# Another issue table and other prices in the planner's account, in a fused attention and gated feed-forward kernel

## The chip, the cores and the metric

The kernel runs on one core of a Trainium2 chip. The metric is the device time of one execution in microseconds (us). Engines are named as the profile names them: PE is TensorE's matmul, PEld its weight load, DVE is VectorE, ACT is ScalarE, POOL is GpSimd, SP is SyncE, which issues most of the DMAs.

## The reference

The input x is 2048 tokens of 512 features, and all is float32. It is normalized over the features, and the normalized rows go through softmax attention with 32 heads of 16 and through a gated feed-forward network with 1792 hidden features. The two results are multiplied and added to the input:

```python
def _A_ref(x, wqkv, wo):                       # H = 32 heads, Dh = 16
    qkv = (x @ wqkv).reshape(B, S, 3, H, Dh) ...
    scores = einsum("bhqd,bhkd->bhqk", q, k) * Dh ** -0.5
    p = softmax(scores, axis=-1)
    return einsum("bhqk,bhkd->bhqd", p, v) ... @ wo

def _B_ref(x, w1, w3, w2):                     # F = 1792
    h = silu(x @ w1) * (x @ w3)
    return h @ w2

xn = layernorm(x)
return x + _A_ref(xn, wqkv, wo) * silu(_B_ref(xn, w1, w3, w2))
```

## The kernel before

**Precision.** A float32 number is split into a rounded part and a remainder ("hi" and "lo", both of the fp32r type), and a product is made of three matmuls: lo x hi, hi x lo, hi x hi. Queries and keys hold the parts of their 16 features stacked on 64 rows, so that one matmul of 64 rows does all three.

**Prologue** (the first 160 us). The input is normalized, transposed and split; queries, keys and values are made from it and written to DRAM; weights stream in.

**Main stage.** Two pieces of work that don't need each other share PE. The first is attention. It goes in 32 phases, two (halves of the queries) for each pair of heads. A phase has 64 units of kind m (lines 388 and 390: a block of scores of 128 queries by 512 keys is made, and VectorE reduces it to row maxima), 64 units of kind s (lines 624 and 627: scores the other way round, with the maximum folded in as two more rows, and ScalarE's exponential), and 16 value blocks v (line 637: four matmuls of 17 columns, one in each quarter of the array's columns, that add the exponentials times the values into one bank called pv). The maxima of a phase come before its exponentials; between them lie a small chain (max_rows: VectorE, ScalarE, VectorE, then a DMA). After a phase, take_out copies pv, and a generator of six steps divides by the sums: DMAs, a reciprocal on VectorE, DMAs again, one multiplication and two splitting instructions on POOL (lines 658 to 662), and the store.

The second is the feed-forward network, in units of kind f (line 855). A product takes 12 (gate, up) or 21 (down) pairs of matmuls, each with half of the 128 rows of the contraction. After a gate product ScalarE takes a tanh and a copy out of the bank, and POOL multiplies; after an up product ScalarE copies, and POOL multiplies and splits into hs. Down products read hs. POOL also splits all weights (lines 320 and 321).

**Lanes.** A matmul of kind f, s or m uses 64 of the array's 128 rows, so two run side by side: a lane for the upper rows and one for the lower. A value block uses all rows.

**The order.** PE's order is written out: ORDER_OF_ISSUE, a string of 8598 letters. A small letter is a half in lane 0, a capital one in lane 1, v a value block, o a piece of the output projection (at the end). The loop at the end of the kernel function reads a letter, first lets side work out (settle, small, tend), and then emits the letter's matmul; a letter that isn't possible yet goes on a list and is tried again at each letter.

**The account.** Whether a letter is possible, which of the seven PSUM banks it takes, and when side work is written into the engines' queues is decided while the program is built, by a class Model that keeps a clock per lane and a "free at" time per engine. SLOT is the time of a half, TURN the time lost between halves and a value block, VALUES the time of a value block, COST the time of a standard piece of work on an engine and DONE what is added until it is known to be done. `mod.work(engine, start, cost)` books work and returns its end. On the chip, every engine runs its own queue in the order written, and semaphores enforce the dependences; a wrong account makes no wrong result, only waits.

Of the kernel before, what the change touches and what calls it, by code (L numbers as in the profile page):

```python
# [62 lines left out]
    "fFMvMsfSMfFsfFmSfFfMFsMffSffMFfFMfsFsFfmFfFFfFMSffMfFsfSmfFFsFmsFfFMsFFfmSfmFFfmFfMMmvvMsMffSFfSfFms"
    "FfFMffSmFFsmFFfSfmFfSFfSfFsFmSsvvSsmMsSvvMsFmSfFfFsFmFsFfSmfFFsmFFsFfMfSffMfFfMSfmMvvvmSMmSsvSFffMSf"
    "fMfSffFMfSfmSFfFsmfSfFMFsfFmsFFfFsmFfFFMsfFmSfFmFFsfMFfsFFmsFFfFmmMfFmSvvsMSmSmvsMMsfMfSvMssMMsvfMfM"
    "sMmMvvMsSffFMffSfMFsfFMfFsmFfSFfmFFsfSfMsFfFmFFffMSfFffMSfsFmFsFFfmSfFmfSFfmFSffFFFmmmFmMvvvvMsmFfSF"
    "sFfFmSFfSfmfFfSMFsFfmsFFMfsFFfMffMfMsMvvvMsMfSffSfFMfSfFmsFfFsFMsFfFmSFffSmfFFsfFmFSSmvvSmFmsFFfSfFm"
    "FsFmsFFffSfMSffFMsfFFmFfSfSfSffMmMvvmMsMmMvvvMfSfMffSSfMfSffMffSfMSffMfsFFMfsFFsfMFfFsfMFsfmFsFFMfsf"
    "FSfmFFsfFMsfFMfFFsmfFSfFmfMFmFfMmvvvMsMmSsvmSSfmFFsfFFmSfFFmMfsFfSffFMsFFfsFmfSFfMfSffMSFfsFfMSffFmF"
    "sFfMsfFFMfFmsFSmvvSmSsmMvSmSfmFFMvvvmSSfmfFfSmfSFmsFfFMfFsSffMfFSfMfFfsFfMsFsFMfFfFsfMFsfFMsfFmFsFfM"  # L70
    "fFfFMsSmvvmSsFmSFmvmSmSmSvmSfSFmFffSFmFsfFSmFfFsmFfSfFMfFsFmsFmFfFsFFmSffFFmfSsFmFMvvSsmFsSmvvMmsSmS"
    "vsMmFsFsFfFFmsFfFfMSfMfFsMffFSfFfMfMfMfmMvvsMfSfMSfFffMfFmSfFSfmFFsfFmFsFmFsFfMfFsFfMMmvvSmsSMmvvmSS"
    "fMffFSffMfSfFmFfSFmFsfFFmsFmFsFfFSfsFMfMsvvsSSmmSvvsMFmsFFfFfSfMfsFsFMfFfFsfMfSfFmSfFSffMfFfFMFFfSff"
    "MfSsmFfFsFmFsFfMsfFFmSffFmFMfmFmMvvvMfSsMfFsFffFFmsFMfsFfFfSmFSfMffFsFMfFfffFMfSfMFfSFfSfmsFsMfFFfmS"
    "FfmFsFFfmFFmmFsMFvvSsMmmMvvfMfSfMMffSFfsfSFmfFsFmsFfFMsfFFsMfFFfFmSmfSmvvvsMsSmMvSmFsmFsFmFFfFsFffSM"
    "fSfsFMfFfmFSfFfSfmMfFsSvvSmSsMsvvSsmMsMvSfMfSffMfFSfSfMfsfFMfSFfmSFfsFmFsfFFmFsFfmFFfMfSFffMsfFsFMfF"
    "sFmFsFfmFSFfmSfFFfmfMFmmMvvvmFSfmFSsfFFfFmFsMfSfFfFmsFFmSfSfFfMffSfFsSvvvFsMSfFmsFfFmsFFfFsmFfSFmFsF"
    "ffMSfFffMFfMfMMsvvSfMfSfMfSfffSfMSffMFsFfmsFfFsFMfFsfFMFsfsMFfFffMMsFfMmvvsMFsMmMvvvsMMffSfSffMfSfMf"
    "SfMfsFfFsMFfsFmfSFfMfSfFmSfFSfmfFSfFmSFfsMFfsFfMFsfFmFsFmFFsFmFmFsSvmmSmMvvMmMmsSvvSmMsSmvmFFsFsmFFs"
    "FmfSfFfMFfsFmFsFmFFsFfmSFfSfmFsfFmSFfMffSfFMfFffMfMfMMfmMvvvmSMsMsFvMsfSfMffSfMfSfMffSfMsfFFsMfFFsmF"  # L80
    "SffMFsfFmFsFFmfSfSFfmfSFfMSffFmFsfFMsFfFFmFmmFmSvvvSssSSsvvvvMsFfFsSmFfFmSFfFsfSmfFfFmSFfmFSfFFsfMFf"
    "sFmfFSmfFfsFFFmsFFfFMsFfmFfFmSfFfSmFSfFfmFsFmFsFfFMfSfSfMsvvvvsMMmsSvmSFsmFSmvsMFffSfMSFffMsfFSmfFSf"
    "FsMfFffMSFffFsmFFfMSFfffMsFmFsFsfFfMFsfFSmFfMfFsfFMfFFmsMsmvvMmmSMvvvmSSmfSFffFFmSFfmfFSfMfSFfmFsfFf"
    "SMFsfFmfFfFFMSfffMSfSffMfsFFmFssFmFFfMfsFFsfFFmmFmMFvvvsMmSsMvSmfMmMvvMssSmfFfFFmsFFfSmFffSfMfSfFmSF"
    "fFfmSFffFFMfSffMSffSfMfFsFmFsFfmFsFmFsFFfmFSmfFMmvvsMsMmMvvMfsMSfmSvSmMssMvSmFmsFFfsFFmSFfFmsFSffMff"
    "SfFMSfFfsMffSFfMffFMffSfSFfMfFsFmsFFfmSfFmFsFFfFmFmmFmSvvSmsMSmvMsfMSfSmvMmSssMvMssFmFmFsFFfFsfFMfsF"
# [58 lines left out]
def kernel(ctx: ExitStack, tc: tile.TileContext, x, wqkv, wo, w1, w3, w2, out):  # L145
    nc = tc.nc
# [148 lines left out]
    mod = Model()  # L295
# [1042 lines left out]
```

## Time and profile before

| | |
|---|---|
| median of 3 runs | 1714.51 us (1714.36 to 1714.62) |
| the profiled execution | 1715.0 us |
| its span, first to last instruction | 1713.2 us |
| granted PE clock | 1.000 |
| busy share: PE, DVE, ACT, POOL | 100%, 84%, 72%, 45% |
| HBM traffic | 89 GB/s over the span |

In the profile, a group or piece of the timeline names its line, the engine, the operation and the tile written and read (`mp<-m` is the reduction of a bank m into mp). A matmul's length in the timeline is its latency; matmuls overlap, so what they cost is read from the distances of their starts. A value block appears as 8 matmul records.

### The profile page before, as it was taken

Reading aid. Unit: us, or ns where it says so; the run is one execution under the profiler, and the core shown is the slowest. Engines: PE = TensorE matmul, PEld = TensorE weight load, DVE = VectorE, ACT = ScalarE, POOL = GpSimd, SP = SyncE. Lnnn points to the kernel's source line nnn. Section 1 sums busy time; section 2 is a strip of 40 time slices with the busy share of each in tenths; the row PEclk is TensorE's granted clock in tenths of the full one; section 3 lists DMA queues with packets and bytes.
Section 4 is the critical chain, followed back from the end, with each engine's and each line's share of the span. In section 5 each row is a group of like instructions: output and inputs, shape, how many; then the busy total and the mean of one; then the engine's idle time right before and its main releaser. Section 6 shows DMA issues by size and latency. Waiting matters only on the chain.

```text
span 1713.2 us, 35632 instructions
## 1 busy us (share of the span) xinstructions
PE 1706.2 (100%) x13204; PEld 1093.8 (64%) x13204; DVE 1447.2 (84%) x2477; ACT 1233.2 (72%) x2408; POOL 764.2 (45%) x793
## 2 busy tenths in 40 slices
PE   9999999999999999999999999999999999999999
PEld 7877666666666666665656666666666656665466
DVE  7567998989898888899979898978999899779835
ACT  4223787787787877787787877887887777778962
POOL 4102754355545560656266525562556336642201
PEclk9999999999999999999999999999999999999999
DMA  8757213132333221232323213233422223131712
GB/s 284 249 205 206 66 40 71 45 76 64 71 105 72 79 55 37 68 69 73 99 80 69 73 30 73 56 70 109 81 59 67 58 55 100 45 106 55 244 61 99
DMA packets 146478, 155.37 MB, mean 91 GB/s; under 512 B 41472, under 2 KB 100864, under 8 KB 143328
## 3 DMA queue, kind: packets, MB, share of 16 engines
q1 hardware_dynamic: 145440, 152.04, 32.1%
q8 instruction: 104, 1.70, 0.4%
q10 hardware_dynamic: 864, 1.05, 0.2%
q14 instruction: 70, 0.57, 0.1%
HBM read 107.97 MB, written 44.02 MB: 89 GB/s over the span
## 4 chain that ended last, share of the span: by engine, by line
PE 97%; DVE 1%; POOL 1%; DMA 1%; issue 0%; SPq 0%; ACT 0%; POOLq 0%; DVEq 0%
PE f L855 27%; PE pv L637 27%; PE m L388 16%; PE e L624 15%; PE m L504 2%; PE e L194 2%; PE e L198 2%; PE e L196 2%; PE o L194 1%; PE o L198 1%; PE o L196 1%; DVE mp L390 1%; PE m L477 0%; DMA ks<-qk 0%; PE o L1086 0%
## 5 line engine op out<-in xcount | busy, mean ns | idle before, releaser
L390 DVE TENSOR_REDUCE mp<-m 128x1 f32<-128x512 f32 x2048 | 1286.4, 683 | 171.7 <-PE m L388 110.9
L627 ACT ACTIVATE pt<-e 128x512 f32<-128x512 f32 x2048 | 1071.5, 605 | 276.6 <-PE e L624 157.0
L624 PE MATMUL e<-qs,ks 64*128 64x512 f32 x2048 | 713.0, 410 | 0.1
L388 PE MATMUL m<-ks,qs 62*128 62x512 f32 x2048 | 710.9, 415 | 0.0
L637 PE MATMUL pv<-pt,vt 128*17 128x512 f32 x4096 | 491.0, 595 | 0.0
L388 PEld LDWEIGHTS m<-ks,qs 62*128 62x128 f32 x2048 | 338.4, 184 | 148.4 <-DVE mp L390 48.6
L624 PEld LDWEIGHTS e<-qs,ks 64*128 64x128 f32 x2048 | 341.5, 184 | 142.9 <-ACT pt L627 48.4
L637 PEld LDWEIGHTS pv<-pt,vt 128*17 128x17 f32 x4096 | 93.7, 96 | 237.0 <-issue 229.8
L855 PE MATMUL f<-xtl,wh 64*128 64x512 f32 x488 | 174.2, 393 | 0.0
L855 PE MATMUL f<-xth,wh 64*128 64x512 f32 x488 | 172.9, 393 | 0.0
L855 PE MATMUL f<-xth,wl 64*128 64x512 f32 x488 | 172.2, 394 | 0.0
L740 POOL TENSOR_TENSOR h<-g,h 128x512 f32<-128x512 f32 x56 | 72.1, 1288 | 213.7 <-ACT h L736 213.5
L855 PE MATMUL f<-wh,hs 64*128 64x512 f32 x496 | 158.1, 393 | 0.0
L855 PE MATMUL f<-xth,xel 64*128 64x512 f32 x408 | 148.9, 394 | 0.0
L855 PE MATMUL f<-xtl,xeh 64*128 64x512 f32 x408 | 148.8, 392 | 0.0
L855 PE MATMUL f<-xth,xeh 64*128 64x512 f32 x408 | 146.1, 392 | 0.0
L855 PE MATMUL f<-xeh,hs 64*128 64x512 f32 x400 | 127.1, 394 | 1.0 <-POOL hs L742 1.0
L321 POOL TENSOR_TENSOR wl<-wr,wh 128x512 fp32r<-128x512 f32 x92 | 118.4, 1287 | 7.7
L320 POOL TENSOR_SCALAR wh<-wr 128x512 fp32r<-128x512 f32 x92 | 56.9, 619 | 109.9 <-PE e L624 59.0
L321 POOL TENSOR_TENSOR xel<-wr,xeh 128x512 fp32r<-128x512 f32 x76 | 97.8, 1287 | 6.3
L855 PE MATMUL f<-wl,hs 64*128 64x512 f32 x248 | 91.1, 391 | 0.0
L855 PEld LDWEIGHTS f<-wh,hs 64*128 64x128 f32 x496 | 85.9, 185 | 6.5 <-issue 2.5
(175 smaller groups left out, 2016.6 us busy)
## 6 DMA issues: line engine op xcount, KB each, us to landing
wr<-in_B_w_dram SPq DMA_DIRECT2D x168, 256.0 KB
qs<-qk SPq DMA_DIRECT2D x186, 64.0 KB
ks<-qk SPq DMA_DIRECT2D x90, 128.0 KB
qk<-sh SPq DMA_DIRECT2D x32, 256.0 KB
qk<-sl SPq DMA_DIRECT2D x32, 256.0 KB
v<-vrow SPq DMA_DIRECT2D x16, 272.0 KB
xin<-in_A_x_dram SPq DMA_DIRECT2D x16, 256.0 KB
g<-part SPq DMA_DIRECT2D x16, 256.0 KB
```

The costliest lines, as they stand in the source:

```text
L194: nc.tensor.matmul(ps, lhs[1], rhs[0], start=first, stop=False)
L196: nc.tensor.matmul(ps, lhs[0], rhs[1], start=False, stop=False)
L198: nc.tensor.matmul(ps, lhs[0], rhs[0], start=False, stop=last)
L320: nc.gpsimd.tensor_scalar(hi, t, 1.0, 1.0, op0=ALU.mult, op1=ALU.mult)
L321: nc.gpsimd.tensor_sub(lo, t, raw(hi))
L388: nc.tensor.matmul(ps, qs[p % 2][64 * h:64 * h + KM, q0:q0 + P], ks[p % 2][64 * h:64 * h + KM, c * 512:(c + 1) * 512], start=True, stop=True)
L390: nc.vector.reduce_max(mp[p, half][:, h, qt, c:c + 1], ps, axis=AX.X)
L624: nc.tensor.matmul(ps, ks[p % 2][64 * h:64 * h + KR, k * P:(k + 1) * P], qs[p % 2][64 * h:64 * h + KR, q0:q0 + 512], start=True, stop=True)
L627: nc.scalar.activation(pt, ps, AF.Exp, scale=DH ** -0.5)
L637: nc.tensor.matmul(pv[32 * j:32 * j + VW, :], vt[2 * p // GH][:, key, 2 * p % GH + j % 2, :], pt, start=key < 2 if last else k == 0, stop= ...
L740: nc.gpsimd.tensor_mul(h2, g, h2)
L855: nc.tensor.matmul(ps, left[r], right[r], start=starts and lane == 0, stop=ends and lane == 1)
```

## The change

Two things change in the text.

1. The table ORDER_OF_ISSUE is replaced as a whole. Both tables have 8598 letters, with the same count of each kind. Counted in the texts:

| in the table | before | after |
|---|---|---|
| f and F, s and S, m and M | 4032, 2048, 1984 | 4032, 2048, 1984 |
| v, o | 512, 22 | 512, 22 |
| runs of neighbouring v | 268 | 253 |
| of these with 1, 2, 3, 4, 5, 6 blocks | 103, 107, 42, 12, 3, 1 | 83, 107, 45, 11, 6, 1 |
| stretches of halves between v or o | 278 | 265 |
| surplus of one lane over the other, added over the stretches | 144 | 150 |
| letters after the last m | 106 | 119 |

2. The account's numbers change, and it gets two bookings that it didn't have: for a phase's outputs, 0.18 on VectorE at the reciprocal and 3.3 on POOL at the multiplication and split. The instructions of these steps are the same.

```diff
 ORDER_OF_ISSUE = (
-    "fMSffMMsSfFfMfSfFsSffMffMfSffSfMSffMsfsFfMsfFMfsFfFMsFfFmSfFFmsFFmmMvMmmFMmvvvSmsMFfSfFffMSffMfSfsFF"
...
-    "sSsoovvosSsSSsovvSsSsSsoosSsSSsvvvsSSssSoSssSSsosSsSSsvvvsSsSsSooSsosSoSsvvSsSsoooSsSssSoooovvvvvv"
+    "FSMfsfMfMSffSMfffSfMSfMfffSfMSfsffMfsMFsFfmFsfFMsfFmFsFFFmsFfMfmMfFsMvvvMsMfSfSfFffMsFFfmFsMfFSffFfM"
...
+    "SvvvSsSsSsoSsSsSsoosSsSsSvvvvvsSsSsSsoooSssSSsvvvSsSssSosSSsSsvvSssSSsooSoossSosoooSvvooosSssSvvvv"
 )

     class Model:
-        SLOT, LOAD, TURN, VALUES, CLEAR, LATENCY, NOTICE = 0.232, 0.1, 0.097, 0.858, 0.983, 0.44, 0.054
-        COST = {"act": 0.495, "dve": 0.605}
-        DONE = {"act": 0.107, "dve": 0.078}
+        SLOT, LOAD, TURN, VALUES, CLEAR, LATENCY, NOTICE = 0.2335, 0.1, 0.097, 0.866, 0.983, 0.44, 0.054
+        COST = {"act": 0.495, "dve": 0.6}
+        DONE = {"act": 0.107, "dve": 0.083}
...
-                self.there[i] = mod.work("pool", mod.now, 1.9) - 0.1
+                self.there[i] = mod.work("pool", mod.now, 1.96) - 0.1
...
                     nc.scalar.activation(th, ps, AF.Tanh, scale=0.5)
-                    mod.work("act", lanes.begins + mod.LATENCY, 0.6)
+                    mod.work("act", lanes.begins + mod.LATENCY)
...
-                        mod.work("pool", ready, 1.9)
+                        mod.work("pool", ready, 1.96)
...
-                        made[i] = mod.work("pool", ready, 3.2)
+                        made[i] = mod.work("pool", ready, 3.3)
...
                         nc.vector.tensor_add(y, y, ps)
-                        free_at[lanes.at_bank[i]] = released[i] = mod.work("dve", ready, 0.7)
+                        free_at[lanes.at_bank[i]] = released[i] = mod.work("dve", ready)
...
-                        soon("pool", mod.work("act", ready, 0.6), i, lambda ready: times(ready, th))
+                        soon("pool", mod.work("act", ready, 0.5), i, lambda ready: times(ready, th))
...
-                        soon("sync", mod.work("pool", ready, 1.9) + 0.3, i, lambda ready: nc.sync.dma_start(
+                        soon("sync", mod.work("pool", ready, 1.96) + 0.3, i, lambda ready: nc.sync.dma_start(
...
             if c[2] == 0:
-                c[0] = mod.work("dve", mod.now, 0.25)
+                c[0] = mod.work("dve", mod.now, 0.15)
             elif c[2] == 1:
                 c[0] = mod.work("act", c[0], 0.2)
             elif c[2] == 2:
-                c[0] = mod.work("dve", mod.now, 1.15)
+                c[0] = mod.work("dve", mod.now, 0.95)
...
                 c[0] = mod.now + (LATER if c[2] < PHASES - 4 else SOON)[c[3]]
+                if c[3] == 1:
+                    mod.work("dve", mod.now, 0.18)
+                elif c[3] == 4:
+                    mod.work("pool", mod.now, 3.3)
...
             nc.scalar.copy(sums[j][0], pv)
-        pv_free = mod.work("act", begins + mod.VALUES + 0.3, 0.6) + mod.NOTICE
+        pv_free = mod.work("act", begins + mod.VALUES + 0.3) + mod.NOTICE
```

More of the change, by code (lines that the diff above doesn't have):

```diff
@@ new lines @@
+    "MfSfmFSfFFsfMSffFmfFSmFsfFFmSFffFmFsFmmSvvsMmMSsvvMsmSsFmFvMmsSsMvvmSsSmMvmSsMFfFffSfMsFffMSfSfFFmFs"
+    "FfmSfFMfsFfFfMfFSfMfSFffMsfmFsFfMFsmFFfsFfMFsFmFfMmfFMFmvvvvmSSFFsmffFmSfFfSmFfSfMsFfFfsMfFFsMffFFfM"
+    "fSfMFfSfSFfmsfFFmfSfMfSFffMsFmFsFFfFmFmFmmMvvvMsmSsMvSmfFsMFfSfFmFsFfSmfFFsMfsFfFMsFfmFFffMfMfSMfSmv"
+    "vmMsMsMvvfMSfMfSfSffMSFffMfSffMfSfMfSfmFsFfsFmFFsfFmSfFMfSfFsfFFmSfFsFmFsfFMSfffFMsfFSmFFfmFFfmMMsvv"
+    "mSmSmSvFmFsSsMmvmMMssMvvvmSFmsFsFFsFmFFfmFFsmfFSfSFfmfFFsmFSffFMsfFfSMfFfSmFFFffMfSSfFMfffMfMMfMfmMv"
@@ new lines @@
+    "vvsMSmsfFfFmsFFmfFSffMSSfMfFsfFffMsFFmFsFfmFSfFmFsFffSMsfFFfMsfFMfFfSffMMsvMmmSSmvvFmmSFsSmvMmsSmSvs"
+    "MFsmFsFmFFsFfFfSmFfFsFmFsfFMffSmFsFFfMfSfmFSffMFfsFFmMsvmMMsMsvvvmSsMmMvvSmmSFfFsFffMFsFfmSfFmFfSfMf"
+    "FsFfMfSFfmFmMFFfmMFvvmSmSfsfFFmsFfFSmfFfSfMsFfFMfSfMffSfSfFfmFFMfFfSmsFfFsMfFFsfMsFFfMsfFfMsFFfFsfFm"
+    "MmMvvvsMMsMsvmSmFSsFmvSmmSMmvvmSfSMfffSfFMSffmFFsFfMsFFsfMffFSmFsfffFMFSfMffFMsfFfSmFFsFmFsFmfFSfmFS"
+    "fFfFsFmSfsMvvMsSsmSvvvvsMFFsmFFsFmFsfFfSmFfSfMffSfFMSffMSffsFFfMFfffMSFFffMsfFsmFSffMFsFfmFsFfMsFFfF"
@@ new lines @@
+    "mFsfSSsvvvmMmMSsvvSmsSmFfFfFFmSffFSfMfsFFmsFfFMfSfSfFmFffFMfSffMfSfMfFSffSmfFSfMsFfFmsFFmFsFfsFFmFsF"
+    "mMvvsMMmmSvvsMFfmSsFFffMSffMfFSfFmSffmFfSfSFFmFfsmFfFFfMfSfSfMfFsFmfFFsFmFsFsMFffMFsFfFmMmFfMmvvvmSs"
+    "MSmFvvMssMMsvvfSMffSfMfSfSfmFsFFmFfFsfMFsSfFmFffFMfFssFmMvmSsMmMvvsMfSfSMffFFmFsFfSmfFsFMsfFFsMfFfSm"
+    "FFfMfMfmFMFsvvMssMffSfFfMSffFsMFfsFFmSffFmSfFmFsFFmfFFfSSfMmvSmSmSmvmSFMsfMMfvvvMffSfMSfSffMfSffMfSf"
+    "MsfmFsFmFfFsFmfFSmfFSfFMfsFffSMsFfFmFsFfMsFfFmFsFMfsFFfMffSMfsSvvvvvSmFsFmFmFsFsFffFSmFfsFfMfFSfMfFs"
@@ new lines @@
+    "MfsFFffMsFFmfSFfFsfMsFFfmSfFfMSffFMfSffMSmvvmMSsSmvvMsMffSSfFffMsFFfmSfFSfmFfFfSmFFsfMfSSFffmFsFmFSf"
+    "FfmFSffSSMfFmfFsFfFmFFmFssvvvsMsMmSvmFFsmFFsFmsFFmsFFFsmFFsFfmfFfSMfFsmFfFsFMSfMfFfsFfMSffMfFsSvMsMs"
+    "MmvvSmmSMmvvmSmFsFFsFfFmSffFMfSfMfFsFffMSfMfsFmFFfFFsfMsMvFvmSmsfFSffmSFFfSmffFSfMFsfMfSfFmSfmFFfFmF"
+    "mMsvvSmMmmMvvvmSfSfMFfSfFmfSFmfFSfmFsFmFFsmFFfSfFfmFfSMfFMsvsMfMsFffSfMfFmSFfFsFmsFfFmFsfFSMffSffMFf"
+    "FfFMSfffSmFsfFMfFFsmFFsfFmSfFmFsfFfMFfmMmMvvvmMsMsMvvMsMsSmvSmFfmSsfFfFSmFFfmSffSfFMSffFmfSFFmsFffMf"
@@ new lines @@
+    "FfFMSfSffFfMFsFmFsFfmFsFFmsFfFmSffFFMffmSmSvsMMssMvvsMMsMsvvMsMssMvSmfMsFfFfSFmsFFSfmFfSfmFfSfFMsFfs"
+    "FfMfSFfMfFfFSfMffSmfSfFMsfFFmsFfFmFSfFmFsfFMfmFmFmMvvvSmSmMmvvmSSmsMvMsFsfMfSFffMSffFsMfFsFFmFfsFfMs"
+    "FmFfSfFfFMFfFSffMfSffFSmsMfsfFFmFsFfMsFsFFfFmsFmMvSmfSfMsMvvvFsMmfSFfSFfSmFfSfmFsfFFmFsFmFsFfMFfSfMf"
+    "SfMfMmvvmMSsMsvvmSfSmFfSFfFmFffSMffSmFsFfFFmSfmFSffFsFmMFfMmvFvvsMSmFfsFffMsFFfMsFfsFMfFsfFsMFfFmfFS"
+    "fMFffMSfMsvMmsSFSmvvMssMMsvfMSffMSfSfMfSffMfSffMSffMffSmsFsFfMfFFsmfFSfMfSfFmSFffSmFFfmSFsfmFsFFfmSF"
@@ new lines @@
+    "fmFFsfFFmMfmFmMvvmSmFSmFmvvmSFsfMFfFsfMfSFfsMfFFsFmsFFffMfSMffSFfFsfMsFMfsFFffMsFSfMfmFfFFfMmfFmMvvv"
+    "mMMssMvvMssFMfsFfFfFmSfFsFFmsFfFfMSfMfFsmFFffSSfFmFfsFFmSfFmfSfFFmSfmFSffFMfSfMfmSvsMmSMmvvmSMmMsvvS"
+    "mmSmSvsMsFmFFsFmFfsFFmfFSFmfFsmFFsFFfsMfsFFmSFffMsFfmFSfMffFmFfMmMvvvSmsSMmvsMFfSfMsfFFmSfFMfsFFsffM"
+    "SFfMfsFmFsFfSfFmSfFmSvvvvmSFsMsFffFFmSFfmSffFFsMfMfSffSfFMfSfFmFfsFfFMffFSfMsFfMsFFfsmFsFfFMFsfFmSfF"
+    "fFFmmfMMsvvMmSmmSvvsMMssMvSmsFFmfSfFfMfSFfmSfsFFmfFMfSfFfMsSfffFFfmFFMFSffFSFfmsmsFFfmFFsFmFsFfMfSfF"
@@ new lines @@
+    "sFffMFfMmMvvvvsMmSfFfsFfMfSfMFffSfMFsFmfsFsFFmFffFSffMFfSfMfSFffMfFsmFsFmFsFFfFmsFmFfSFffMFfSmSmvvsS"
+    "sSmmSsvvvSSmSvvmSFsmFFsmFFfsFFffSFmMfSffSfFMfsFSffMFffFfFMSffMSFffMfFssmFffSFmfSFmSFfFmFsfFmFFfmMmSv"
+    "FvvFvmSsmfFsFfMsfFMfsFFfMsFffMSfSFfsMfFfffMFfFFMfSSFffFmsmFsfFFmFsFsFmFSffMFfmFfSfMfmSvMmMmSmvvvsMsM"
+    "sMvMsMsfFfFSffMfsFMFfsmFfFsFfMSFfFfsMfsFfMFffFMfFFSfSffMsmFfFFsmFFsmFsFfMfSfFmFfMmFfSmvvMsmSmSvvsMMs"
+    "sMvsmSmFSFffFFmFsfFSmFfSfMfsFFfMsFfFmFfMfSfSfMfMFsvmMMmSsvvMmMsmSvvMfSffMfSfMfSfSfMffSfMfSfMfSfFsmFf"
@@ new lines @@
+    "SfFmfSFmFsfFfFSmsFFmFfSfFfSmFfSFmfSfFmFsFfMsFFfmFfMFmFmMvvvvvSmFsmfSFfFmFFsSfmFMffSFfsfFfMFsFMffSFfs"
+    "mFSffFMFsFfmSfFmFsFfFsFMffSffSfMmSvMmsSMsvvMsmMMsSvvsMsMsvvSmFsmFFfsFFmFsFmFffSFmFsfMFFsfMFfSffMFsff"
+    "MSfFMfsFSffMfSfFmSFfMfsFFfSfMfmFmMvvvSFmfSmfFfSFmsFfFFmFsmFfSFmFfFsfFFsmFfSFmsFFfFmSfFmFfFmSfSmvvmSM"
+    "mSmvvMsFmsFFffSFmFsFfMfsFfMfSmFfFSffMfSFfFmfMmFMmFvvMssfMFfsFfMFfmSffMSFfsFfMFfsFsfFMFsfffMFfFMFSfff"
+    "FMsfsFMsFfFmFsFfMfSfsFMfFFsmFfFsmMvSmMmmSvvmMSmmSvvvsMMmsSvSmmFsFFsfFFmfSFffSMfFsFmsFFffSMfSfMfFfffF"
@@ new lines @@
+    "MSffMfSSffFMfSfmFSffMFfsFmFsFFmsFFmFfmFFssMvvSsMmsMvvSsMmsMvvSmfMFsFfsFfMfSFfmSFfsFfMSfFfSmfFFmsFfFF"
+    "ffMSffFMSffMFfsFsmSffFFmSfFsMFfmFsFsFfFfFmSSmvvvvvvMssFfFfMFfsFMfFsfMfFSffMfSMfFsfFFsfMFsFfFMfSFfmfs"
+    "FfFFmfFSFmfSMffsFFmmFsfFfSFSsfFSsmvvvMSsSvSfmFFsFmFsFfmFSfmFfFfSmFmSfFfSfSFffMSffMffFfSFMffSfMsfFmFs"
+    "FMfsFFfmFsFFmsFMfFfSmFfmMvvMmsMmMvvvsMsMsMvMsffSMFsfFfMFffSmsFFmFSfFfMfsfFfSMfsFfFmFffFFMSfSfmFFmfSf"
+    "sFFmFfSfmSfFmFsFfFFsFsfMmSvvvMssMSmvSmMfsFsFFffMSfFfsMfFfSFmsFFfmSfFMfsFFffMmFfMFmFMvvmSfMSfMsvSmmSm"
@@ new lines @@
+    "SvvvmSMfSfSfffMfSfSMfffSMfsfMsFfFsMfFfFsMFfsFmsFfFMsFfsFMffFSmFsFfMsFFfmfSFmFsFFfffMfMMMsvvSmmMsMvvS"
+    "mfSFfFmSfFfmSFffSmFfSfFSmFffFmSsFfFmFFsfMSffFmFfSFmfSFmfFsFFmsFFffMMfSfmSFvvvvvsMSsmFffFfMFsfMFsfFFm"
+    "SffMsFFfFsFmsFFmFsFfSfmFSffMSffFFmSfSfFmfMfFSffFMfMsvMmmSsSvvsMMmSsvMsmFFssmFfFFsFFmFsfFmFSfFsmFFfsF"
+    "mFsFFmfFsFFmfFfMfMfSfMfMMfvvvsMMmSsvmSfMfSFsFfFmfSfFmSfFmFSfmFFfSfFmFsMffFFmMfMsvvMsMsmMvvsMfSfMfFSf"
+    "fMfSfFsMfFfSfMFsFfmSfFsFmfFFsFmFFfFmSFfsfMFsFfMsFFfmSFfFfmSfmFSfMFfFfsmFMmvvsMmSmMvvmSsMMsvmSfFSmSff"
@@ L137 @@
+    "mSsMSmvsMsSMSomSSsSsSvvMssMMsoSMsSsSvvsMSMmsSvsSMsmoMSvmSMmSSsvvsMMsmSSvSsSmSmMvvSssSSssSSssSvSossSs"
+    "SvvvSsSsSsoSsSsSsoosSsSsSvvvvvsSsSsSsoooSssSSsvvvSsSssSosSSsSsvvSssSSsooSoossSosoooSvvooosSssSvvvv"
 )
```

118 lines of the change are left out of this document (34 added, 84 removed).

## The prediction

> **What bounds the kernel now.** I read the head of the page first, then the chain of work that ended last, then the stage in which the issue table is at work (from 165 to 1600 us), and only then single matmuls.
>
> ```profile
> span 1713.2 us, 35632 instructions
> PE 1706.2 (100%) x13204; PEld 1093.8 (64%) x13204; DVE 1447.2 (84%) x2477; ACT 1233.2 (72%) x2408; POOL 764.2 (45%) x793
> ...
> PE 97%; DVE 1%; POOL 1%; DMA 1%; issue 0%; SPq 0%; ACT 0%; POOLq 0%; DVEq 0%
> ```
>
> ```profile
> 165.00:1600.00 1435.00, 1433.87 (x11737) 900.32 (x11734) 1273.59 (x2172) 1121.99 (x2186) 722.98 (x740) 1.00 0.28 72
> ```
>
> ```profile
> by line: PE f L855 32.4%; PE pv L637 30.2%; PE m L388 17.9%; PE e L624 17.0%; DVE mp L390 0.7%; DMA ks<-qk 0.3%; POOL xel L321 0.2%; issue 0.2%; DMA qs<-qk 0.1%; POOL hs L742 0.1%; POOL ol L662 0.1%; POOL g L725 0.1%; POOL ot L658 0.1%; POO
> ```
>
> The second fence is the stage by engine (PE, PEld, DVE, ACT, POOL, then clock, DMA share, GB/s), the third the chain inside it. PE is idle for 1435.00 - 1433.87 = 1.1 us of the stage, at a full clock of 1.00. The four matmul lines make 97.5% of the chain there; the row reductions (DVE mp) make 0.7% of 1435 us, which is 10.0 us, and the transfers of keys and queries 0.4%, which is 5.7 us. So an order can win only in two ways: by making the same matmuls follow each other more closely, or by taking from these few us.
>
> A busy PE isn't a packed PE, so the next view is the timeline of PE around one run of value blocks (start, length, what, count).
>
> ```profile
> 500.98 0.39 PE L388 MATMUL m<-ks,qs 62*128 62x512 f32 x1
> 500.99 0.39 PE L624 MATMUL e<-qs,ks 64*128 64x512 f32 x1
> 501.31 1.05 PE L637 MATMUL pv<-pt,vt 128*17 128x512 f32 x8
> 502.30 0.49 PE L388 MATMUL m<-ks,qs 62*128 62x512 f32 x1
> 502.30 0.50 PE L624 MATMUL e<-qs,ks 64*128 64x512 f32 x1
> 502.63 0.40 PE L855 MATMUL f<-xth,wl 64*128 64x512 f32 x1
> 502.64 0.39 PE L624 MATMUL e<-qs,ks 64*128 64x512 f32 x1
> 502.87 0.39 PE L855 MATMUL f<-wh,hs 64*128 64x512 f32 x1
> 502.87 0.40 PE L388 MATMUL m<-ks,qs 62*128 62x512 f32 x1
> 503.10 0.39 PE L855 MATMUL f<-xeh,hs 64*128 64x512 f32 x1
> 503.11 0.40 PE L855 MATMUL f<-xtl,wh 64*128 64x512 f32 x1
> ```
>
> Half-array matmuls start in pairs, one on each half of the rows. Undisturbed, the next pair starts 0.23 us later (502.64, 502.87, 503.10): a letter of the table that stands for a half costs 0.115 us. The last pair before the value block is followed only after 501.31 - 500.98 = 0.33 us, 0.10 too many, and the first pair after it only after 502.63 - 502.30 = 0.33, again 0.10 too many. A stretch of halves between value blocks thus costs 0.20 us beside its letters. What the value blocks themselves cost is seen in the chain's pieces (start, length, blocks of 8 records):
>
> ```profile
> 1368.31 2.70 PE pv L637 x24
> ...
> 1337.10 3.56 PE pv L637 x32
> ...
> 1491.26 4.42 PE pv L637 x40
> ...
> 1688.51 5.28 PE pv L637 x48
> ```
>
> Three, four, five and six blocks take 2.70, 3.56, 4.42 and 5.28 us: 0.86 a block, and 2.70 - 3 x 0.86 = 0.12 us once a run. The single block above fits: 502.30 - 501.31 = 0.99 = 0.86 + 0.13. So one more run of value blocks, with its stretch of halves, costs 0.12 + 0.20 = 0.32 us of PE, whatever is in it. That's the price list.
>
> **The change part by part.** No instruction is added or removed: both tables hold the same letters (2016 + 2016 f, 1024 + 1024 s, 992 + 992 m, 512 v, 22 o). The account's numbers cost nothing on the chip; they only decide which bank is taken, and where side work is written into the queues. The work ahead of the table (the first 160 us) is written out in the same order by the same code. Counting the letters of the two tables gives the rest.
>
> (1) Runs of value blocks: 268 become 253. 15 x 0.12 = 1.8 us less.
>
> (2) Stretches of halves (cut by v or o): 278 become 265. 13 x 0.20 = 2.6 us less.
>
> (3) Lanes out of balance. In a stretch with more capitals than small letters (or the reverse) one half of the array stands empty for the odd ones. The surplus, added over all stretches, goes from 144 to 150 letters. Each is worth between nothing (the neighbour fills it) and a whole 0.23; I take half of that, 6 x 0.115 = 0.7 us more, with 0 and 1.4 as ends.
>
> Together: -1.8 - 2.6 + 0.7 = -3.7 us.
>
> The Trainium skill bears on the price of a switch: "TensorEngine Tiling (Array Packing)", Tiling Modes, says that a change of tiling mode (not of tile) drains TensorE, and "TensorE: Matmul & The Clock Gate", Part 2, puts a drain at about 128 cycles. By these pages, as an estimate, two drains of 128 cycles at 2.4 GHz are 0.11 us a run, 15 runs are 1.6 us, and the time would be 1712.9 us. The trace agrees that a switch costs, but shows 0.32 us where the pages give 0.11.
>
> (4) Waits for the engines that empty the banks. VectorE and ScalarE have these rows:
>
> ```profile
> 499.44 1.28 DVE L390 TENSOR_REDUCE mp<-m 128x1 f32<-128x512 f32 x2
> 500.95 8.27 DVE L390 TENSOR_REDUCE mp<-m 128x1 f32<-128x512 f32 x13 [0.24 <-PE e L624]
> ```
>
> ```profile
> 1425.70 6.79 DVE mp L390 x11
> ```
>
> ```profile
> L390 DVE TENSOR_REDUCE mp<-m 128x1 f32<-128x512 f32 x2048 | 1286.4, 683 | 171.7 <-PE m L388 110.9
> L627 ACT ACTIVATE pt<-e 128x512 f32<-128x512 f32 x2048 | 1071.5, 605 | 276.6 <-PE e L624 157.0
> ```
>
> Two reductions of 0.683 us take 1.28 together, so they start 0.60 apart. VectorE is busy for 1273.59 of 1435 us (88.8%), and waits for PE oftener than PE for it. The longest place where it leads is the one at 1425.70, eleven reductions in 6.79 us. Whether the new table crowds the reductions more can be counted: give each letter its time on PE by the price list and each m 0.60 us of VectorE. In stretches of 60 letters (about 9 us) VectorE's demand passes PE's time by over 1 us at 69 starting places in the old table and 66 in the new; in stretches of 120 letters at 15 and 7; in stretches of 30, at 131 and 152. Short crowds are slightly commoner, long ones rarer. The seven banks bridge the short ones. Of the 10.0 us in which reductions lead, I take 0.5 off; the ends are half of them off (-5.0) and as much again on (+10.0).
>
> (5) POOL charged for a phase's outputs (3.3 at the multiplication and split), 1.96 for 1.9, 3.3 for 3.2. Three instructions a phase have been in POOL's queue all along; now the account knows, so hidden products are called done later and their consumers placed later.
>
> ```profile
> POOL ot L658 <- DMA rb<-rd: 39.9, 3, 25.3
> ```
>
> ```profile
> PE f L855 <- POOL hs L742: 1.0, 1, 1.0
> ```
>
> ```profile
> PEld f L855 <- POOL hs L742: 1.4, 1, 1.4
> ```
>
> POOL once stood 25.3 us behind a transfer with everything queued after it, but PE lost 1.0 us to its products in the whole run, and a weight load waited 1.4 us. So the better account can win at most 2.4 us here. Placing a consumer later than needed costs nothing while other letters fill PE. I take 0, with -2.4 and +2.4 as ends.
>
> (6) ScalarE's and VectorE's small work is charged less (0.495 for 0.6, 0.15 for 0.25, 0.95 for 1.15, 0.6 for 0.7): at nothing, hidden by ScalarE's idle time (1435 - 1122 = 313 us). Without that cover, it would show as waits of the score matmuls for ScalarE. Transfers: the DMAs of a phase leave after the same fixed delays, and the DMA share is 0.28. The 5.7 us of transfers on the chain may move either way; I take 0, ends -5.7 and +5.7.
>
> (7) The last stretch, after the final m: 68 s, 18 v, 20 o become 78 s, 22 v, 19 o. ScalarE needs 10 x 0.50 = 5.0 us more there, PE 5 pairs x 0.23 + 4 x 0.86 + 2 runs x 0.32 = 5.2 us more, so ScalarE doesn't become the bound.
>
> ```profile
> 1612.00:1660.00 48.00, 48.00 (x296) 26.42 (x293) 25.66 (x45) 34.37 (x69) 0.00 (x0) 1.00 0.48 155
> ```
>
> In that stage ScalarE is busy for 34.37 of 48 us. The PE time is already in (1) to (3); I add 0.
>
> Sum: -3.7 - 0.5 = -4.2 us. The profiled execution took 1715.0 us, its span of 1713.2 and 1.8 around it, which the change doesn't touch; it would take 1710.8. It lies 0.5 us above the median of the runs, 1714.51, so the forecast for the median is **1710.3 us**, 0.24% less. A measurement of this kernel tells about 0.2%, 3.4 us, from no change: below 1711.1 is faster, above 1717.9 slower. The forecast lies only 0.8 us inside.
>
> **The rivals.** *The banks take the gain.* PE's pairs then wait for a bank where they waited for a switch before. For it: VectorE at 88.8%, short crowds up from 131 to 152. Against it: VectorE's own idle time before reductions is 171.7 us, and 110.9 of that is spent waiting for PE. Between half and all of the 4.2 us is lost: 1712.4 to 1714.5, within 0.2%. If VectorE were the bound throughout, its work would be the same in any order and the time 1714.5. "TensorEngine Tiling (Array Packing)", PSUM Bottleneck, in the Trainium skill states this rule: tiling makes TensorE faster but not the emptying of PSUM, which may become the bottleneck. By it the gain would vanish here; the trace bears it out only in stretches like the one at 1425.70.
>
> *The table isn't followed.* A letter that the account doesn't find possible is put off, and put off letters can cut the value runs again. Every run that returns costs 0.32; with five more, 4.2 - 1.6 = 2.6 us are left, 1711.9. The old order shows few cuts of that kind: on the chain, pieces of 24 to 48 records stand uncut. It ends within 0.2%.
>
> *Slower: crowded reductions.* This is the mechanism at 1425.70 in more places. At the upper end of (4) the reductions lead for 20 us in place of 10, and the time is 1714.5 - 3.7 + 10.0 = 1720.8. It turns slower than before when they lead for more than 3.7 us beyond the 10.0, and by over 0.2% from 7.1. Against it: long crowds are rarer in the count.
>
> *More gain.* With half of the reductions' 10.0 us gone: 1714.5 - 3.7 - 5.0 = 1705.8.
>
> **How the numbers follow.** The forecast with its neighbours from 1708.0 to 1711.1 has 0.54; more gain 0.08; the banks take the gain 0.20; the table isn't followed 0.10; slower 0.08. That gives 0.62 faster, 0.30 within 0.2%, 0.08 slower. The range leaves out the slower case and most of the largest gain: it goes from 1707.0 to 1714.8. The likeliest case's own range, by the ends of (3) and some 2 us of (4) to (6), is 1708.0 to 1712.5.
>
> **What would show it.** The chain should keep its 97% of PE, and the three-block piece should stay at 2.70 us. In the stage from 165 to 1600 the same work should be done earlier: the last m and the last gate product should start some 3 to 4 us sooner. Steps (1) and (2) are wrong if the pairs beside a value block are 0.23 apart. Step (4) is wrong if DVE mp L390 on the chain leaves 0.7% by more than 0.3. Step (5) is wrong if PE waits for POOL's hs for over 2 us. The prediction falls if 15 fewer runs are there and the time isn't, or if the executed runs aren't 15 fewer.

## The result, and the profile after

The changed kernel takes 1709.87 us (median of 9 runs, 1708.91 to 1710.93); the kernel before, run beside it, 1714.42 (9 runs, 1714.11 to 1714.85). The ratio is 0.9973, with a 95% interval from 0.9963 to 0.9984. That is 4.55 us less, where 4.2 less, 1710.3, was forecast. The profiled execution took 1709.36 us, with a span of 1707.5.

The head of the page and the chain of the changed kernel:

```profile
span 1707.5 us, 35607 instructions
PE 1701.6 (100%) x13204; PEld 1099.8 (64%) x13204; DVE 1441.7 (84%) x2477; ACT 1229.6 (72%) x2408; POOL 764.5 (45%) x793
...
PE 99%; DVE 1%; DMA 0%; SPq 0%; ACT 0%; issue 0%; DVEq 0%; ACTq 0%
```

The stage from 165 to 1600 us, by engine, and the chain inside it:

```profile
165.00:1600.00 1435.00, 1435.00 (x11773) 907.93 (x11770) 1277.28 (x2184) 1121.87 (x2192) 725.86 (x742) 1.00 0.29 72
```

```profile
by line: PE f L855 33.3%; PE pv L637 31.0%; PE m L388 18.2%; PE e L624 17.4%; PE o L1086 0.1%; issue 0.0%
```

In the same 1435 us PE gets through 11773 matmuls where it did 11737, so 36 more. The chain now has nothing but PE in it: the 0.7% of the row reductions and the 0.4% of transfers are gone. It's tempting to call that the gain; the experiments say it isn't.

The timeline of PE around a run of value blocks, and the chain's pieces of 3, 4 and 5 value blocks:

```profile
501.06 0.40 PE L624 MATMUL e<-qs,ks 64*128 64x512 f32 x1
501.38 1.05 PE L637 MATMUL pv<-pt,vt 128*17 128x512 f32 x8
502.37 0.49 PE L388 MATMUL m<-ks,qs 62*128 62x512 f32 x1
502.37 0.49 PE L855 MATMUL f<-wh,hs 64*128 64x512 f32 x1
502.70 0.40 PE L624 MATMUL e<-qs,ks 64*128 64x512 f32 x1
502.71 0.39 PE L855 MATMUL f<-wl,hs 64*128 64x512 f32 x1
502.94 0.39 PE L855 MATMUL f<-wh,hs 64*128 64x512 f32 x1
```

```profile
1404.19 2.70 PE pv L637 x24
...
1639.05 4.42 PE pv L637 x40
...
1684.57 3.56 PE pv L637 x32
```

The prices of a switch haven't moved: 0.32 from the last pair to the value block (0.09 too many), 0.99 for one block, 0.33 to the second pair (0.10 too many), 2.70, 3.56 and 4.42 us for three, four and five blocks. What changed is how often they are paid. The planner puts off a letter that isn't possible yet, and the letters that PE is really given form 249 runs of value blocks and 257 stretches of halves, against 265 and 274 before: 16 and 17 fewer, where the two tables as written had 15 and 13 fewer. The surplus of one lane, as given, goes from 76 to 72 letters; as written it went from 144 to 150.

Adding up the distances between starts in the two traces, from the first value block of the table to the last matmul, gives where the time went. In value blocks PE spent 472.5 us before and 470.5 after: 2.0 less, where 16 x 0.12 is 1.9. In stretches of halves it spent 1009.8 and 1007.3: 2.5 less, where 17 x 0.20 = 3.4 were to be saved, so 0.9 went to something else there. The output projection's pieces took 0.5 less. Together that's 5.0 us. The rest of the two spans' difference, 5.7, is the start of the first value block, at 169.0 and 168.3 us; in the traces of the experiments it lies anywhere from 168.1 to 169.9, so it is scatter. A pair of traces thus fits the medians' 4.55 us only to about 1 us.

### The profile page after: what moved, and what is told of

Read it like the earlier page. It is cut to its first block, busy times and chain, and to the rows that moved or that the text cites. A ratio compares the mean times of both kernels' runs of the same rounds, so it can differ in the third digit from the quotient of the medians.

```text
span 1707.5 us, 35607 instructions
## 1 busy us (share of the span) xinstructions
PE 1701.6 (100%) x13204; PEld 1099.8 (64%) x13204; DVE 1441.7 (84%) x2477; ACT 1229.6 (72%) x2408; POOL 764.5 (45%) x793
## 4 chain that ended last, share of the span: by engine, by line
PE 99%; DVE 1%; DMA 0%; SPq 0%; ACT 0%; issue 0%; DVEq 0%; ACTq 0%
PE f L855 28%; PE pv L637 28%; PE m L388 16%; PE e L624 16%; PE m L504 3%; PE e L194 2%; PE e L198 2%; PE e L196 2%; PE o L194 1%; PE o L198 1%; PE o L196 1%; PE m L477 0%; DMA wr<-in_A_wqkv_dram 0%; PE o L1086 0%; DVE pt L1032 0%; DVE wr L1033 0%
## 5 line engine op out<-in xcount | busy, mean ns | idle before, releaser
L624 PEld LDWEIGHTS e<-qs,ks 64*128 64x128 f32 x2048 | 346.1, 184 | 128.5 <-DVE mp L390 32.9
L855 PE MATMUL f<-wh,hs 64*128 64x512 f32 x496 | 153.6, 393 | 0.0
L855 PE MATMUL f<-xth,xel 64*128 64x512 f32 x408 | 144.2, 394 | 0.0
```

The lines of the kernel that those rows point to most:

```text
L624: nc.tensor.matmul(ps, ks[p % 2][64 * h:64 * h + KR, k * P:(k + 1) * P], qs[p % 2][64 * h:64 * h + KR, q0:q0 + 512], start=True, stop=True)
L855: nc.tensor.matmul(ps, left[r], right[r], start=starts and lane == 0, stop=ends and lane == 1)
```

## Experiments

Two theories stood at the start. Theory P (packing) is the prediction's: fewer switches, each at its price. Theory W says that the better account takes away waits, and the smaller number of runs goes along with it.

### Table and account apart

```diff
 ORDER_OF_ISSUE = (
-    "fMSffMMsSfFfMfSfFsSff...
+    "FSMfsfMfMSffSMfffSfMS...            # e1: this alone
...
-        SLOT, LOAD, TURN, VALUES, ... = 0.232, 0.1, 0.097, 0.858, ...
+        SLOT, LOAD, TURN, VALUES, ... = 0.2335, 0.1, 0.097, 0.866, ...   # e2: this, and all the other prices and bookings, alone
```

> The new table with the account of before (its prices, and no booking for a phase's outputs). Written out by the planner, PE gets 250 runs of value blocks and 258 stretches of halves (before: 265 and 274; the changed kernel: 249 and 257). Theory P (packing: the time follows from how often PE switches, 0.12 us a run of value blocks and 0.20 us a stretch of halves): 1714.4 - 15 x 0.12 - 16 x 0.20 = 1709.4, give or take 1. Theory W (the better account takes away waits, and the smaller number of runs goes along with it): without the new account the gain is lost, 1713.5 to 1715.

> The old table with the account of the changed kernel: 265 runs, 274 stretches, as before. Theory P: 1714.4, give or take 1. Theory W: most of the gain is there, 1710 to 1711.

Measured: the new table with the old prices takes 1714.00 us (10 runs; before 1714.19; ratio 0.9999, 0.9990 to 1.0008). The old table with the new prices takes 1714.59 (10 runs; ratio 1.0002, 0.9993 to 1.0012). So each half alone is worth nothing that shows, and together they are worth 4.55 us. Both theories fall in their plain form: e1 has 250 runs of value blocks and gains nothing, and e2 has the whole new account and gains nothing.

The chain of e1 in the stage from 165 to 1600 us:

```profile
by line: PE f L855 33.5%; PE pv L637 30.9%; PE m L388 18.2%; PE e L624 17.3%; PE o L1086 0.1%; DVE mp L390 0.0%; issue 0.0%
```

It is as clean as that of the changed kernel, and the time is that of the kernel before. The chain's share for the reductions is therefore no measure of this gain.

In e1 the letters that PE is given differ from those of the changed kernel at 11 places, in 20 of 8662 letters (a letter that moves counts where it leaves and where it comes); but only 745 of the 4340 bank choices are the same. By the sums of starts, its value blocks took 471.1 us (0.6 more than in the changed kernel, and still 1.4 less than before), and its stretches of halves 1011.5, 4.2 more. Nearly all of the loss is in the halves.

### Which part of the account

```diff
-                self.there[i] = mod.work("pool", mod.now, 1.96) - 0.1     # e5: 1.96 and 3.3 back to 1.9 and 3.2,
+                self.there[i] = mod.work("pool", mod.now, 1.9) - 0.1
-                if c[3] == 1:                                             #     and no booking of a phase's outputs
-                    mod.work("dve", mod.now, 0.18)
-                elif c[3] == 4:
-                    mod.work("pool", mod.now, 3.3)
...
-                    mod.work("act", lanes.begins + mod.LATENCY)           # e6: 0.6, 0.25, 1.15 and 0.7 again
+                    mod.work("act", lanes.begins + mod.LATENCY, 0.6)
...
-        COST = {"act": 0.495, "dve": 0.6}                                 # e7: SLOT, VALUES, COST, DONE as before
+        COST = {"act": 0.495, "dve": 0.605}
```

> The changed kernel with the POOL prices of before and without the two bookings for a phase's outputs; everything else as changed. PE's letters come out in exactly the same order; 3657 of 4340 bank choices stay. If what the words of the change say is what makes the account fit (theory A), the gain is gone as in the run with all old prices: 1714. If POOL hardly matters to PE (theory B, step 5 of the prediction), the gain stays: 1709.9, give or take 1.

> The changed kernel with only the old prices of ScalarE's and VectorE's other work (tanh and copies 0.6, the maxima's rows 0.25 and 1.15, the add 0.7). 250 runs, 258 stretches, 26 letters come out at another place, 1024 of 4340 bank choices stay. Theory C (these prices decide which bank is taken and which letter is late): most of the 4.1 us that the run with all old prices lost, 1712.5 to 1714. By step 6 of the prediction: 1709.9, give or take 1.

> The changed kernel with only the old SLOT, VALUES, COST and DONE (0.232, 0.858, 0.605, 0.078). 249 runs, 257 stretches, 9 letters at another place, 851 bank choices stay. Theory D (the traced spacings make the account fit): 1712 to 1714. Theory C: under 1711.5.

Measured: 1709.63 us for e5 (9 runs; ratio 0.9973, 0.9963 to 0.9983), 1713.88 for e6 (10 runs; 0.9997, 0.9988 to 1.0007), 1711.49 for e7 (10 runs; 0.9983, 0.9974 to 0.9992). POOL's prices and bookings are worth nothing that shows, as theory B said. The prices of ScalarE's and VectorE's other work are worth 4.0 us, as much as all prices together in e1, and the constants 1.6: theory D's 1712 is missed, and theory C's 1711.5 is met by a hair. The parts don't simply add up: set side by side by their value blocks, e1 and e6 lose their time at much the same places.

Where e6 loses its time is seen by setting the value blocks of the two traces side by side, first with first. The distance grows from 0.3 to 2.8 us at block 480 and 4.5 at block 496, and two places make 2.8 of these 4.2 us: 1.1 us between the value blocks at 1314 and 1325 us of the changed kernel, and 1.7 in the tail around 1620. The rest is spread over places of less than 0.4 us each. In e1 the same two places make 1.2 and 1.7 us.

The first place in the changed kernel (PE, then SyncE, which issues the transfers):

```profile
1324.28 0.71 PE L388 MATMUL m<-ks,qs 62*128 62x512 f32 x4
1324.92 1.48 PE L637 MATMUL pv<-pt,vt 128*17 128x512 f32 x12
```

```profile
1316.26 2.84 SPq L367 DMA_DIRECT2D ks<-qk  x6
1319.20 0.36 SPq L673 DMA_DIRECT2D o<-oh  x1
...
1324.42 0.30 SPq L673 DMA_DIRECT2D o<-ol  x1
```

and in e6 (PE, the weight loads, VectorE, SyncE):

```profile
1326.21 0.44 PE L388 MATMUL m<-ks,qs 62*128 62x512 f32 x2
1327.38 0.50 PE L388 MATMUL m<-ks,qs 62*128 62x512 f32 x2 [0.74 <-DVE mp L390]
1327.81 1.05 PE L637 MATMUL pv<-pt,vt 128*17 128x512 f32 x8
```

```profile
1327.35 0.21 PEld L388 LDWEIGHTS m<-ks,qs 62*128 62x128 f32 x2 [1.15 <-DVE mp L390]
```

```profile
1326.64 1.93 DVE L390 TENSOR_REDUCE mp<-m 128x1 f32<-128x512 f32 x3 [0.42 <-PE m L388]
```

```profile
1318.10 0.52 SPq L673 DMA_DIRECT2D o<-oh  x1
...
1321.58 0.42 SPq L673 DMA_DIRECT2D o<-ol  x1
1322.10 2.69 SPq L367 DMA_DIRECT2D ks<-qk  x6
```

The same four m stand ahead of a value block. In the changed kernel all four go at once. In e6 the third m comes 1.17 us after the first. The profile puts this wait down to VectorE, but VectorE had nothing left to read when it began: it stood idle for 0.42 us until the first of these four m, and the reduction that began at 1326.64 reads that m's own bank. By the program's order the third m is the first that reads the next pair's keys. Ahead of its weight load stand two instructions that wait for transfers:

```profile
L388 PEldq EVENT_SEMAPHORE  x2: 51/51/51, 1327.2 to 1327.3; - x2
```

The first of them runs at 1327.16, just after the last packet of the third of the six key transfers (ks) has landed at 1327.14; one lane's m needs three of the six. e1 separates the two causes, by its chain:

```profile
1326.65 0.69 DVE mp L390
1327.34 0.21 issue
1327.55 0.50 PE m L388 x2
```

There VectorE's reduction is over at 1327.34, and the m still waits 0.21 us more; the third key transfer landed at 1327.30, and the instruction that waits for it ran at 1327.33. So PE waits for the keys. In the changed kernel their transfers are issued from 1316.26 and the third has landed at 1321.61, over 2 us before the m; the eight stores of a phase's outputs (o) come behind them. In e6 and e1 the eight stores come first, and the keys are issued 4.0 us after the first store. The key transfers are issued at a letter of the table, the stores by the account's clock, so the account decides which goes first. In e5 and e7 the keys go first, and the distance doesn't grow at this place.

The second place is in the tail. PE in the changed kernel:

```profile
1617.02 0.96 PE L624 MATMUL e<-qs,ks 64*128 64x512 f32 x6
...
1620.90 0.96 PE L624 MATMUL e<-qs,ks 64*128 64x512 f32 x6
1621.80 1.05 PE L637 MATMUL pv<-pt,vt 128*17 128x512 f32 x8
```

and in e6, with a weight load of the value block:

```profile
1619.82 1.68 PE L624 MATMUL e<-qs,ks 64*128 64x512 f32 x8
1621.59 1.53 PE L637 MATMUL pv<-pt,vt 128*17 128x512 f32 x8
```

```profile
1622.08 0.12 PEld L637 LDWEIGHTS pv<-pt,vt 128*17 128x17 f32 x4 [0.37 <-ACT pt L627]
```

In the changed kernel an output piece of 12 matmuls stands between the two groups of six scores (1617.02 and 1620.90), and ScalarE's exponentials run under it. In e6 the piece wasn't possible by the account and came later: eight scores follow each other, and the value block waits for their exponentials and stretches to 1.53 us, 0.48 too many.

### The price of a run, of a merge and of an odd letter

```diff
-    ... v v f F s S M f S m f F ...          # e3: at 32 places a value block is moved
+    ... v f F s S M f S m v f F ...          #     behind the next 8 to 14 letters
...
-    ... v S m M m S m v v v ...              # e4: at 16 places of the old table
+    ... S m M m S m v v v v ...              #     a short stretch leaves the gap between two runs
...
-    ... s S f v v M s ...                    # e8: 24 single letters are moved
+    ... s S v v f M s ...                    #     behind the run that follows
```

> The changed kernel with 32 more runs: at 32 places where two or more value blocks stand together ahead of a long stretch of halves, the last block is moved behind the next 8 to 14 letters, with as many letters of each lane on both sides. 281 runs and 289 stretches. Theory P: 32 x 0.32 = 10.2 us more than the changed kernel, 1720.1. The planner's own account says 15.2 us more, 1725.1. Theory W: a switch gives VectorE and ScalarE time to empty banks, so much of it comes back: under 5 us more, below 1715.

> The kernel before, account and all, with 16 runs merged into a neighbour: a short stretch of 6 to 10 halves between two runs is moved ahead of the first run or behind the second. 249 runs and 258 stretches, as in the changed kernel. Theory P, if only the count matters: 1714.4 - 16 x 0.32 = 1709.3. Theory W, and the planner's own account, which books waits for banks at the merged places: no gain or a loss, 1714 to 1726, 11.6 us more being the account's own figure.

> The changed kernel with 24 single f or m letters moved behind the run of value blocks that follows them, so that the stretches on both sides are out of balance by one letter: the surplus written out goes from 72 to 120, runs and stretches stay 249 and 257. Step 3 of the prediction took half a pair a letter: 48 x 0.115 = 5.5 us more, 1715.4, with 0 (1709.9) and 48 x 0.23 = 11 (1720.9) as ends. The planner's account says 16.0 us more, 1725.9, since a letter moved also changes which banks are free.

Measured: e3 1724.47 us (4 runs; before 1714.19; ratio 1.0059, 1.0044 to 1.0074), e4 1725.94 (4 runs; 1.0068, 1.0053 to 1.0083), e8 1723.98 (4 runs; before 1714.38; 1.0054, 1.0039 to 1.0069).

In e3 theory P's 1720.1 is missed, and theory W's 1715 by more. A run split off costs (1724.47 - 1709.87) / 32 = 0.46 us. Its value-block part is on the list: 474.5 us against 470.5, where 32 x 0.12 is 3.9. The halves' part is 1018.1 against 1007.3, 0.34 a stretch where the list has 0.20. A letter out of balance costs (1723.98 - 1709.87) / 48 = 0.29 us, above the upper end of 0.23; but a letter that moves also changes which banks are free, as the expectation says, and nothing here tells the two apart. And a merge, which by the list saves 0.32, costs 11.75 / 16 = 0.73 us. So the count of runs alone doesn't give the time. The planner's account was close in all three: 15.2 us for 14.6, 11.6 for 11.75, 16.0 for 14.1.

One merged stretch of 14 letters in e4, PE, then VectorE and ScalarE:

```profile
1036.96 0.50 PE L388 MATMUL m<-ks,qs 62*128 62x512 f32 x1
...
1038.25 0.49 PE L388 MATMUL m<-ks,qs 62*128 62x512 f32 x1 [0.32 <-DVE mp L390]
...
1039.93 1.05 PE L637 MATMUL pv<-pt,vt 128*17 128x512 f32 x8
```

```profile
1037.50 3.68 DVE L390 TENSOR_REDUCE mp<-m 128x1 f32<-128x512 f32 x6 [1.08 <-PE m L388]
```

```profile
1037.63 3.05 ACT L627 ACTIVATE pt<-e 128x512 f32<-128x512 f32 x6
```

Seven pairs should take 7 x 0.23 + 0.20 = 1.8 us, and take 1039.93 - 1036.96 = 2.97. The stretch asks for six reductions (3.68 us) and six exponentials (3.05 us), and there are seven banks; ScalarE also has a copy of pv to make at its start. A value block takes none of the seven: under it, the two engines empty banks while PE works. Where it is taken away, PE waits for what they would have done under it. Both tables have many short stretches of three m and three s between value blocks, which fits this; why they stand there is not shown. This is one of the sixteen places; whether the others are alike stays open.

### How much of it is VectorE

```diff
-        nc.vector.reduce_max(mp[p, half][:, h, qt, c:c + 1], ps, axis=AX.X)
+        nc.vector.reduce_max(mp[p, half][:, h, qt, c:c + 1], ps[:, :256], axis=AX.X)
...
-        nc.scalar.activation(pt, ps, AF.Exp, scale=DH ** -0.5)
+        nc.scalar.activation(pt, ps, AF.Exp, scale=0.1 * DH ** -0.5)
```

> The kernel before with each row reduction over the first 256 of a bank's 512 columns, and the exponential's scale a tenth (the maxima are then of half the keys, and the output is another; every instruction is still there, in the same order). VectorE's reductions become shorter, some 0.4 us for 0.68. The chain gave reductions the lead for 10.0 us. Theory V (banks that VectorE frees late are what PE waits for): 5 to 12 us less, 1702 to 1709. Theory S (PE waits for ScalarE and for its own switches): under 3 us less, above 1711.

> The changed kernel with the same two edits. The price list with the counts that PE is really given says 16 x 0.12 + 17 x 0.20 = 5.3 us less than the shortened kernel before. Theory V: the difference comes close to that, 4.8 to 6. If the account's fit is worth the same with short reductions as without, the difference stays 4.5.

> The kernel before with 16 runs merged, and the same two edits. With full reductions the merging cost 11.8 us, where the price list says 5.1 us less: 16.9 us of waits. Theory V: the waits go, and the merged kernel is 2 to 5 us faster than the shortened kernel before. Theory S: most of them stay, and it is still 6 to 12 us slower.

> The changed kernel with 32 runs split, and the same two edits. With full reductions the splitting cost 14.6 us, 0.46 a run, where the price list says 10.2. Theory V: 9.5 to 11 us more than the shortened changed kernel. Theory S: still 13 to 15.

The group of reductions in e9, to compare with 1286.4 us busy and 683 ns each:

```profile
L390 DVE TENSOR_REDUCE mp<-m 128x1 f32<-128x256 f32 x2048 | 811.9, 421 | 616.2 <-PE m L388 378.2 <-PE e L624 143.2 <-PE f L855 68.7
```

Measured: e9 1708.02 us (4 runs; before 1714.51; ratio 0.9962, 0.9947 to 0.9977), e10 1703.79 (4 runs; 0.9937, 0.9923 to 0.9952), e11 1718.51 (9 runs; 1.0023, 1.0013 to 1.0033), e12 1716.38 (10 runs; 1.0011, 1.0002 to 1.0020).

Taking 475 us of work off VectorE saves 6.5 us in the kernel before and 1709.87 - 1703.79 = 6.1 in the changed one. Theory V holds for that: VectorE's lateness costs some 6 us. But it costs the same in both, so the gain isn't from there. The difference between the two kernels stays 4.2 us with short reductions, as with long ones; the expected 4.8 to 6 wasn't reached. And the merged kernel stays 10.5 us slower than e9, the split one 12.6 slower than e10. For the merged kernel theory V falls; the split one lies between the two theories. With VectorE's part shortened, ScalarE still fills the merged stretch. The same stretch in e11, PE and ScalarE:

```profile
1033.61 0.49 PE L388 MATMUL m<-ks,qs 62*128 62x512 f32 x1
...
1036.56 1.05 PE L637 MATMUL pv<-pt,vt 128*17 128x512 f32 x8
```

```profile
1034.27 3.05 ACT L627 ACTIVATE pt<-e 128x512 f32<-128x512 f32 x6
```

It takes 1036.56 - 1033.61 = 2.95 us, where it took 2.97, and the six exponentials their 3.05.

## Why the prediction was right, and where it wasn't

**The time** (1710.3 forecast, 1709.87 measured, inside its likeliest range) and the direction were right, and the gain shows where it was looked for, in the value blocks and in the halves between them. But the switches don't carry it alone: e1 has 250 runs and 258 stretches, almost those of the changed kernel, and gains nothing. "The prediction falls if 15 fewer runs are there and the time isn't" is what happened in e1.

That the sum came so close is in part luck. For the halves it forecast 2.6 - 0.7 + 0.5 = 2.4 us less, and 2.5 were measured, but none of the three terms fits by itself, as the steps show. The output pieces' 0.5 us less was not in the sum.

**Step 1, runs of value blocks** (1.8 us): 2.0 measured, at 0.12 a run. **Step 2, stretches of halves** (2.6): the list gives 3.4 for the 17 fewer that PE was really given. Counting letters as written missed the ones that the planner puts off. 2.5 is what the halves really gave, with the next two steps in it.

**Step 3, balance** (0.7 more): the sign was wrong, since the balance as given improves from 76 to 72. The price may have been too low as well: a moved letter cost 0.29 in e8 where 0.115 was taken, perhaps with other waits in it.

**Step 4, waits** (0.5 less): the halves show 0.9 more beside the list, and the experiment with short reductions shows no difference of VectorE's waits (6.5 and 6.1 us). The step read a possible gain out of the chain's 0.7%. That share went to nothing, which by the prediction's own mark makes the step wrong, and it did so also in e1, which gained nothing.

**Step 5, POOL at nothing**: confirmed by e5. **Step 6, the small prices at nothing, hidden by ScalarE's idle time**: this is the step that failed. The prices aren't instructions, and ScalarE's idle time hides nothing here. They decide which bank a matmul takes, which letter is put off, and when side work such as a phase's stores goes into a queue. With the old ones under the new table 4.0 of the 4.55 us are gone: 1.1 because the keys are sent behind the stores, 1.7 in the tail, the rest in small pieces. The same step took the transfers at nothing because they leave after the same fixed delays; but these delays run by the account's clock, and the order of the transfers changed with it. The constants (SLOT, VALUES, COST, DONE), worth 1.6 us in e7, have no term in the sum. The prediction set the account's edits to zero one by one, as though the table's gain stood without them. It came out right because the change brings a table together with the account that it fits.

**Step 7, the tail at nothing**: the changed order holds there, but e6 shows 1.7 us lost in it when one output piece is put off.

**The rivals.** That the table isn't followed is what e1 and e6 show, a few letters put off; but the price isn't the run that returns (one, 0.32 us), it is the wait for the keys' transfers and the exponentials that pile up. That the banks take the gain happened in e4, where it cost 16.9 us over the list (11.75 + 5.1). The rule of the Trainium skill beside that rival ("TensorEngine Tiling (Array Packing)", PSUM Bottleneck) agrees with e4, where emptying the banks sets the pace, and not with the change as a whole. The drain of the Trainium skill ("TensorE: Matmul & The Clock Gate", Part 2), from which 0.11 us a run and 1712.9 us were estimated, is too small for the 0.32 that the changed kernel's trace shows again. The crowding that would have made the change slower, and the larger gain, didn't come. **The marks:** the chain's PE share rose from 97% to 99%, and the three-block piece stayed at 2.70 us. The reduction of the last m starts at 1616.1 us where it started at 1627.3, 11 us sooner and not the 3 to 4 forecast: the new table puts more scores behind it (78 for 68), so that mark was a bad one. The last gate product's tanh starts 4.2 us sooner, at 1501.3 for 1505.5, about as forecast. PE doesn't wait for POOL's hs any more (1.0 us before).

What stays open: where in the halves the changed kernel loses its 0.9 us; why a split stretch costs 0.34 and not 0.20 at each place. e12 brings it to 0.27 ((1010.3 - 1001.5) / 32), so VectorE is a part of it. Neither the bank choice nor the place of the stores was tried alone, with everything else of the account kept.

## What to carry to other kernels

A price taken from a trace around one switch (here 0.12 + 0.20 us) is a price at fixed waits: it forecast the difference between two orders that were each made with a fitting account, and failed with the wrong sign where runs were merged by hand. Where an account of the engines decides at build time on buffers, on what is put off and on when transfers are issued, the account is part of the order: change the two together, and take a reversed test of each before saying which of them gained. A clean chain doesn't prove that a stall was worth something; e1's was as clean as the faster kernel's. And the engine that a profile names for a wait can be the wrong one where a transfer lands at the same moment: look at what else the instruction waits for.

## What the runs showed of the hardware

Under a block of value matmuls the engines that empty PSUM could catch up. In the merged stretch of e4, with seven banks and no such block between them, six reductions and six exponentials took 2.97 us of PE time in place of 1.8, and making the reductions 0.26 us shorter each (421 ns for 683) left it at 2.95. Of the 475 us that the shorter reductions took off VectorE's busy time, 6.5 us reached the total, though VectorE was 84% busy.

The first three of the six key transfers landed about 1 us apart, in the changed kernel at 1319.53, 1320.62 and 1321.61 us, the third 4.3 us after it was issued at 1317.30. In e6, behind eight stores, the third was issued at 1322.97 and landed 4.2 us later.
